# Query casts moved from GpSimd to VectorE, and a last tile's stores over two queues in place of three

## The chip, the core and the metric

The kernel runs on one core of a Trainium2 chip. A core has engines that run side by side, each through its own list of instructions in program order: TensorE (PE in the profile; it multiplies matrices, and PEld is its loading of weights), VectorE (DVE) and GpSimd (POOL) for elementwise work, ScalarE (ACT) for functions such as exp and GELU, and SyncE (SP), which here only issues transfers. Transfers (DMA) run beside the engines. The metric is the time of one execution on the device in microseconds, as the median of several runs.

## The reference

Two stages, in float32. Attention in a window of 32 positions to either side, for 8 batches of 8 heads, 576 positions and 64 features a head; then a feed-forward layer over all 4608 tokens.

```python
# q, k, v: (8, 8, 576, 64)
scores = np.matmul(q, k.transpose(0, 1, 3, 2)) / np.sqrt(64)
scores = np.where(np.abs(pos[:, None] - pos[None, :]) <= 32, scores, -1e9)
attn = softmax(scores)                                # written out in the original
x = np.matmul(attn, v).transpose(0, 2, 1, 3).reshape(4608, 512)
h = x @ w_in                                          # w_in:  (512, 2048)
g = 0.5 * h * (1 + np.tanh(c * (h + 0.044715 * h * h * h)))   # c = sqrt(2 / pi)
out = g @ w_out                                       # w_out: (2048, 512)
```

## The kernel before

The tokens are taken in 9 tiles of 512 (t = 0 to 8). In each tile a first product, `ffn_in`, makes h from the attention's output xT and puts it through GELU; a second product, `ffn_out`, multiplies by w_out. From tile 1 on the second product is done as seven half-size products in place of eight (Winograd's form), for which VectorE makes sums of quarters of g (S1 to S4) and combines the results into the output quarters C11, C12, C21 and C22. The attention of batch t + 1 is woven into the second product of tile t, by a plan of steps: s is a group of scores and its exp, m the mask, v the product with V and the reciprocal of the sums, x the scaled write into xT.

Queries and keys arrive in float32. They must be cast to float16 and turned, so that features lie on partitions. From batch 2 on the turning is done by DMA transposes, which SyncE issues:

```python
    def cast_and_turn(b):
        cast_open(b)
        q16, k16 = halfs[b]
        qr, kr, qt, kt = raws[b]
        # ...
        def queries(src, dst, p0, p1):
            for pr in range(NPAIR):                     # 4 pairs of heads
                nc.gpsimd.tensor_copy(
                    dst[:, pr, :, :, :].rearrange("p j h d -> p h j d"),
                    src[:, 2 * pr:2 * pr + 2, :].rearrange("p h (j d) -> p h j d", j=4))
            nc.sync.dma_start_transpose(QTs[b].rearrange("d r j p -> d (r j) p")[:, :, p0:p1],
                                        dst.rearrange("p r j h d -> p (r j h d)"))

        queries(qr, q16, 0, 128)
        for pr in range(NPAIR):
            nc.vector.tensor_copy(k16[:, pr, :, :, :], kr[:, :, 2 * pr:2 * pr + 2, :])
            nc.sync.dma_start_transpose(
                KTs[b % 2][:, pr, 0:512].rearrange("d (c p) -> d c p", c=4),
                k16[:, pr, :, :, :].rearrange("p c h d -> p (c h d)"))
        queries(qt, qt16, 128, 144)                     # the last 64 positions
        nc.vector.tensor_copy(kt16.rearrange("p r h d -> p (r h d)"), kt.rearrange("p h d -> p (h d)"))
        nc.sync.dma_start_transpose(
            KTs[b % 2][:, :, 512:576], kt16.rearrange("p r h d -> p (r h d)"))
```

Queries come as 128 partitions x 512 elements a pair of heads (qr) and 16 x 512 for the tail (qt). The order of the program in one tile decides what stands behind what on each engine:

```python
    for t in range(NT):
        b = t + 1
        att = b < B
        if t:
            for fc in range(begun):
                ffn_in(t, fc, 3, 4)
            if att and b > 1:
                cast_and_turn(b)
            for fc in range(begun, NF):
                ffn_in(t, fc)                           # GELU, and the sums after every fourth
        # ...
        if t and b + 1 < B:
            load_qk(b + 1)                              # SyncE: qr, four parts of kr, qt, kt
        for i in range(113 if t else 65):
            for act in plan.get(i, "").split():
                # s, m, v, x of the plan; with the first v:
                #   if t and g < 0 and b + 1 < B: load_v(b + 1)   # GpSimd: five casting loads
                ...
            # one matmul of the second product
        # ffn_last(t): the last quarter's additions and its stores
```

The scores of a pair need its part of QT and KT (line 354 of the kernel); the sums are line 490:

```python
    def gelu(t, n):
        fc = column(t, n)
        nc.scalar.activation(gTs[t][:, fc, :], phs[fc], AF.Gelu_apprx_tanh)
        if t and n % 4 == 3:
            sums(t, n // 4)

    def sums(t, i):
        # ...
        for dst, x, y, op in ((S1, A21, A22, ALU.add), (S2, S1, A11, ALU.subtract),
                              (S3, A11, A21, ALU.subtract), (S4, A12, S2, ALU.subtract)):
            nc.vector.tensor_tensor(dst, x, y, op=op)
```

Results go out from GpSimd's queue, in the last tile over several queues. `three` is used for the quarter C22 of the last tile alone; there `store` makes two transfers for the first block of 128 tokens and five for the second:

```python
    turn_about, three = [nc.sync, nc.scalar], [nc.sync, nc.gpsimd, nc.scalar]

    def store(t, t4, yo, cols=slice(0, 512), eng=None):
        # for each stretch of rows that is contiguous in the output:
            if t == NT - 1 and eng is None:
                turn_about.append(turn_about.pop(0))
            if eng is three:
                three.append(three.pop(0))
            q_ = three[0] if eng is three else eng or (turn_about[0] if t == NT - 1 else nc.gpsimd)
            q_.dma_start(out_v[b, j, q0 + p:q0 + p + e, cols], yo[m:m + e, cols])
    # ...
        elif n == 4:                                    # in ffn_out
            if not end:
                nc.vector.tensor_tensor(C22, py, U3, op=ALU.add)
            else:
                for x, part in enumerate((py[:, 0, :], pys["apart"][:, 0:256])):
                    nc.vector.tensor_tensor(C22[:, x, :], part, U3[:, x, :], op=ALU.add)
                    store(t, 2 + x, yo[:, 2 + x, :], right, three)
```

Of the kernel before, what the change touches and what calls it, by code (L numbers as in the profile page):

```python
# [29 lines left out]
def cut(b):  # L30
    return 120 if b else 128
# [30 lines left out]
def kernel(  # L62
# [9 lines left out]
    nc = tc.nc  # L72
# [5 lines left out]
    NT = NTOK // 512  # L78
# [149 lines left out]
    for i in (0, 3, 4, 1, 2):  # L228
        m, off = masks[i], 0
# [16 lines left out]
    def cast_open(b):  # L246
        halfs[b] = [hp.tile([128, NPAIR, 4, 2, 64], FP16, name="q16"),
                    hp.tile([128, NPAIR, 4, 2, 64], FP16, name="k16")]
        QTs[b] = ap_.tile([128, NPAIR, 4, 144], FP16, name="QT")
# [44 lines left out]
    def bank(i):  # L294

        return psM.tile([128, 512], FP32, name="mm", tag=f"x{i}")
# [5 lines left out]
# [4 lines that stand above are left out]
        qt16 = hp.tile([16, NPAIR, 4, 2, 64], FP16, name="qt16")  # L306
        kt16 = hp.tile([64, NPAIR, 2, 64], FP16, name="kt16")
        def queries(src, dst, p0, p1):
            for pr in range(NPAIR):
                nc.gpsimd.tensor_copy(  # L310
                    dst[:, pr, :, :, :].rearrange("p j h d -> p h j d"),
                    src[:, 2 * pr:2 * pr + 2, :].rearrange("p h (j d) -> p h j d", j=4))
            nc.sync.dma_start_transpose(QTs[b].rearrange("d r j p -> d (r j) p")[:, :, p0:p1],
# [8 lines that stand above are left out]
        queries(qt, qt16, 128, 144)  # L322
# [3 lines that stand above are left out]
# [132 lines left out]
    def first(t):  # L458

        return (t + 1) % 2  # L460
# [17 lines left out]
    def combine(i):  # L478
        dst, x, y = wino["todo"][i]
        nc.vector.tensor_tensor(dst, x, y, op=ALU.subtract)  # L480
# [11 lines left out]
    out_v = out.rearrange("(b p j) f -> b j p f", b=B, j=4)  # L492
    pys = {}

    turn_about, three = [nc.sync, nc.scalar], [nc.sync, nc.gpsimd, nc.scalar]

    def store(t, t4, yo, cols=slice(0, 512), eng=None):
        m = 0
        while m < 128:
            b, c = divmod(t * 512 + t4 * 128 + m, S)  # L500
            q0, n = (0, cut(b)) if c < 4 * cut(b) else (cut(b), 144 - cut(b))
            j, p = divmod(c - 4 * q0, n)
            e = min(n - p, 128 - m)
            if t == NT - 1 and eng is None:
                turn_about.append(turn_about.pop(0))
            if eng is three:
                three.append(three.pop(0))
            q_ = three[0] if eng is three else eng or (turn_about[0] if t == NT - 1 else nc.gpsimd)
            q_.dma_start(out_v[b, j, q0 + p:q0 + p + e, cols], yo[m:m + e, cols])  # L509
            m += e  # L510

    later = []
# [1 line left out]
    def ffn_out_0(t4, fc):  # L514
        if fc == 0:
            pys[t4] = bank(t4 % 2)
        nc.tensor.matmul(pys[t4], gTs[0][:, fc, t4 * 128:t4 * 128 + 128], w_out16[:, fc, :],
                         start=(fc == 0), stop=(fc == NF - 1))
        if fc == NF - 1:
            yo = yp.tile([128, 512], FP32, name="yo", tag="yo")  # L520
            nc.vector.tensor_copy(yo, pys[t4])
            if t4 == 3:
                store(0, t4, yo)
            else:
                later.append((t4, yo))

    def ffn_out(t, i):

        n, blk, f = i // 16, i // 8 % 2, i % 8
        if t == 1 and i > 2 and i in wino["todo"]:  # L530
            combine(i)
        a, w, new = WINO[n]
        end = t == NT - 1
        if i % 16 == 0 and new:
            pys[n % 2] = bank((first(t) + n) % 2)
            if end and n == 4:
                pys["apart"] = psO.tile([128, 512], FP32, name="py2", tag="O")
        py = pys[n % 2].rearrange("p (b c) -> p b c", b=2)
        apart = end and blk and n in (4, 6)
        if a[0] == "A":  # L540
            r0, c0 = 8 * (int(a[2]) - 1) + f, 256 * (int(a[1]) - 1) + 128 * blk
            lhsT = gTs[t][:, r0, c0:c0 + 128]
        else:
            lhsT = wino[a][:, f, 128 * blk:128 * blk + 128]
        one = end and n in (4, 6)
        nc.tensor.matmul(pys["apart"][:, 0:256] if apart else py[:, blk, :], lhsT,  # L546
                         wino[w][:, f, :], start=(new and i % (8 if one else 16) == 0),
                         stop=(i % (8 if one else 16) == (7 if one else 15)),
                         skip_group_check=True)
        if i % 16 < 15:  # L550
            return
        yo, left, right = wino["yo"], slice(0, 256), slice(256, 512)
        C11, C12, C21, C22 = (yo[:, r:r + 2, c] for r in (0, 2) for c in (left, right))

        M1, U2, U3 = C21, C12, C22
        if n == 0:
            nc.vector.tensor_copy(M1, py)
        elif n == 1:
            nc.vector.tensor_tensor(U2, py, M1, op=ALU.add)
        elif n == 2:  # L560
            nc.vector.tensor_copy(C11, py)
            if end:
                for x in range(2):
                    store(t, x, yo[:, x, :], left, nc.sync)
        elif n == 3:
            nc.vector.tensor_tensor(U3, py, M1, op=ALU.add)
        elif n == 4:
            if not end:
                nc.vector.tensor_tensor(C22, py, U3, op=ALU.add)
            else:  # L570
                for x, part in enumerate((py[:, 0, :], pys["apart"][:, 0:256])):
                    nc.vector.tensor_tensor(C22[:, x, :], part, U3[:, x, :], op=ALU.add)
                    store(t, 2 + x, yo[:, 2 + x, :], right, three)
        elif n == 5:
            nc.vector.tensor_tensor(C21, py, M1, op=ALU.add)  # L575
            for x in range(2):
                store(t, 2 + x, yo[:, 2 + x, :], left if end else slice(0, 512))
# [121 lines left out]
    for t in range(NT):  # L699
        b = t + 1  # L700
# [18 lines left out]
        for i in range(113 if t else 65):  # L719
# [33 lines left out]
            if t == 0 and i in (38, 40, 55):  # L753
                t4, yo = later.pop(0)
                store(0, t4, yo, eng=nc.scalar)
            if t == 0 and i < 64:
                ffn_out_0(*ORDER_0[i])
            elif t and i < 112:
                ffn_out(t, i)
# [36 lines left out]
```

## Time and profile before

| what | value |
|---|---|
| time, median of 3 runs | 315.29 us (314.19 to 315.38) |
| span of the profiled execution | 313.6 us |
| TensorE busy | 298.4 us, 95% |
| VectorE busy | 204.2 us, 65% |
| ScalarE busy | 200.3 us, 64% |
| GpSimd busy | 133.8 us, 43% |
| granted TensorE clock | 0.998 of full |
| end of VectorE's last addition | 308.83 us |

The profile is of one execution. Its times start at the first instruction and run to 313.6; a row of a time line gives start, duration, engine, line of the kernel, operation and what is written and read, and in brackets the idle time of the engine before it with what ended it. "xN" joins N instructions of a kind that follow each other; two that overlap in the pipeline start closer together than one lasts. "SPq" is SyncE issuing transfers. Groups give total busy time and then the mean in nanoseconds of one. An engine that isn't the bound may idle for nothing; what counts is idle time of the one that sets the end.

### The profile page before, as it was taken

What the parts mean: (1) busy time and instruction counts of PE and PEld (TensorE: products, weight loads), DVE (VectorE), ACT (ScalarE), POOL (GpSimd) and SP (SyncE); (2) the same over time, 40 slices, a digit from 0 to 9 for tenths busy, and PEclk for the clock granted to TensorE, in tenths of its full rate; (3) what the DMA queues carried; (4) which work ended last, traced back from release to release, by engine and by line L of the source; (5) the groups of instructions that cost most, each with busy time, mean ns of one, the idle gap of its engine ahead of it and who ended that gap; (6) DMA issues with size and microseconds to landing.
All of it is one profiled execution on the core that took longest, in us unless ns stands there. A gap on an engine that the chain in (4) does not pass through costs nothing.

```text
span 313.6 us, 6733 instructions
## 1 busy us (share of the span) xinstructions
PE 298.4 (95%) x2643; PEld 187.4 (60%) x2643; DVE 204.2 (65%) x405; ACT 200.3 (64%) x315; POOL 133.8 (43%) x209
## 2 busy tenths in 40 slices
PE   7789989998899999999999999999999999999993
PEld 2453535444685478547864786477646864784582
DVE  5664587749776866696669666966686653633551
ACT  1677467567667677767776867686768676706600
POOL 3557255099108910892079306930680051006001
PEclk9999999999999999999999999999999999999999
DMA  7999998999996899769975999599653022004013
GB/s 207 238 332 372 374 333 194 281 176 139 123 268 142 121 116 253 171 120 138 246 178 111 134 238 193 107 125 260 145 135 78 2 64 73 2 0 134 2 43 92
DMA packets 120035, 50.64 MB, mean 161 GB/s; under 512 B 101351, under 2 KB 113296, under 8 KB 120004
## 3 DMA queue, kind: packets, MB, share of 16 engines
q1 hardware_dynamic: 84243, 37.43, 53.4%
q0 software_dynamic: 34864, 11.63, 38.2%
q10 hardware_dynamic: 897, 1.16, 1.1%
q8 instruction: 20, 0.33, 0.5%
q14 instruction: 11, 0.09, 0.1%
HBM read 37.62 MB, written 9.44 MB: 150 GB/s over the span
## 4 chain that ended last, share of the span: by engine, by line
PE 71%; SPq 12%; DMA 12%; DVE 2%; issue 1%; ACT 1%; POOL 0%; DVEq 0%
PE mm L546 31%; PE mm L446 19%; PE ph L446 11%; SPq L139 5%; PE ps_o L387 4%; PE ps_s L354 4%; DMA KT<-k 3%; DMA wst<-in_moe_w_in_dram 3%; DMA qr<-in_q_dram 3%; PE ps_d L387 3%; SPq L162 2%; DMA kr<-in_k_dram 2%; SPq L130 1%; SPq L181 1%; DVE k L318 1%; SPq L185 1%
## 5 line engine op out<-in xcount | busy, mean ns | idle before, releaser
L509 POOL DMA_DIRECT2D out_dram<-y x80 | 43.7, 554 | 129.3 <-DVE y L575 110.9
L446 PEld LDWEIGHTS <-w_in 128*128 128x128 f16 x576 | 56.1, 98 | 66.6 <-POOL w_in L190 1.8
L446 PE MATMUL mm<-xT,w_in 128*128 128x512 f16 x352 | 86.4, 379 | 0.2 <-POOL w_in L190 0.2
L454 ACT ACTIVATE gT<-mm 128x512 f16<-128x512 f32 x88 | 52.4, 599 | 36.7 <-PE mm L446 36.7
L446 PE MATMUL ph<-xT,w_in 128*128 128x512 f16 x224 | 58.8, 379 | 0.3 <-POOL w_in L190 0.3
L490 DVE TENSOR_TENSOR s<-gT 128x512 f16<-128x512 f16 x64 | 34.6, 541 | 35.3 <-ACT gT L454 35.1
L546 PEld LDWEIGHTS <-s 128*128 128x128 f16 x512 | 48.6, 98 | 7.5
L360 ACT ACTIVATE pe<-ps_s 128x704 f16<-128x704 f32 x64 | 43.4, 729 | 9.8 <-PE ps_s L354 9.0
L546 PE MATMUL mm<-t,s 128*128 128x256 f16 x376 | 45.7, 273 | 0.0
L401 ACT ACTIVATE lt<-ps_d 128x480 f32<-128x480 f32 (+3 forms) x40 | 22.3, 556 | 32.1 <-PE ps_d L387 32.0
L454 ACT ACTIVATE gT<-ph 128x512 f16<-128x512 f32 x56 | 33.0, 599 | 13.0 <-PE ph L446 12.9
L546 PEld LDWEIGHTS <-gT 128*128 128x128 f16 x384 | 36.0, 98 | 7.3
L546 PE MATMUL mm<-w_out,gT 128*128 128x256 f16 x256 | 32.8, 273 | 0.0
L369 DVE TENSOR_TENSOR pe<-pe,mask 128x704 f16<-128x704 f16 x64 | 31.3, 526 | 1.0 <-ACT pe L360 1.0
L411 DVE TENSOR_TENSOR xT<-ps_o,lt 128x480 f16<-128x480 f32 (+5 forms) x38 | 20.2, 549 | 13.5 <-ACT lt L402 13.5
L387 PEld LDWEIGHTS <-V 128*64 128x64 f16 x336 | 18.0, 109 | 11.6 <-issue 4.4
L402 ACT ACTIVATE lt<-lt 128x480 f32<-128x480 f32 (+3 forms) x40 | 23.5, 587 | 1.3
L490 DVE TENSOR_TENSOR s<-s,gT 128x512 f16<-128x512 f16 x32 | 23.2, 726 | 1.1
L387 PE MATMUL ps_o<-pe,V 128*64 128x160 f16 (+2 forms) x244 | 21.7, 241 | 1.2 <-POOL V L263 1.2
L87 ACT ACT_TABLE_LOAD x17 | 21.8, 1283 | 1.1 <-PEq L780 0.8
L387 PE MATMUL ps_d<-pe,ones 128*64 128x192 f16 (+2 forms) x264 | 22.4, 235 | 0.0
L170 POOL DMA_DIRECT2D V<-in_v_dram x24 | 21.5, 916 | 0.0
(77 smaller groups left out, 322.0 us busy)
## 6 DMA issues: line engine op xcount, KB each, us to landing
kr<-in_k_dram SPq DMA_DIRECT2D x32, 256.0 KB, 7.7
qr<-in_q_dram SPq DMA_DIRECT2D x6, 1024.0 KB, 8.4
V<-in_v_dram POOLq DMA_DIRECT2D x30, 128.0 KB, 6.2
wst<-in_moe_w_in_dram SPq DMA_DIRECT2D x3, 1024.0 KB
wst<-in_moe_w_out_dram SPq DMA_DIRECT2D x3, 1024.0 KB, 11.2
qr<-in_q_dram SPq DMA_DIRECT2D x8, 256.0 KB
vr<-in_v_dram SPq DMA_DIRECT2D x16, 128.0 KB, 5.2
out_dram<-y POOLq DMA_DIRECT2D x24, 48.0 KB, 2.0
```

The costliest lines, as they stand in the source:

```text
L87: nc.scalar.add_instruction(mybir.InstLoadActFuncSet(name=nc.get_next_instruction_name(), act_func_set_id=which, ins=[], outs=[]))
L170: nc.gpsimd.dma_start(V[:, c, :, :], v[b, :, 128 * c:128 * c + 128, :].rearrange("h p d -> p h d"))
L360: nc.scalar.activation(pe, ps[:, :, 0:w], AF.Exp, scale=SCALE)
L369: nc.vector.tensor_tensor(pe, pe, m.rearrange("p (o w) -> p o w", o=1).broadcast_to(list(pe.shape)), op=ALU.mult)
L387: nc.tensor.matmul(bk[r0:r0 + 64, at:at + 4 * n].rearrange("d (j p) -> d j p", j=4)[:, :, p0 - q0:p1 - q0], V[:, c, 2 * pr + h, :] if w == ...
L401: nc.scalar.activation(lt[:, 0:n], d[:, 0:n], AF.Ln)
L402: nc.scalar.activation(lt[:, 0:n], lt[:, 0:n], AF.Exp, scale=-1.0)
L446: nc.tensor.matmul(ph, w_in16[:, dc, fc * 128:fc * 128 + 128], xT[:, dc, t * 512 % RING:t * 512 % RING + 512], start=(dc == 0), stop=(dc = ...
L454: nc.scalar.activation(gTs[t][:, fc, :], phs[fc], AF.Gelu_apprx_tanh)
L490: nc.vector.tensor_tensor(dst, x, y, op=op)
L509: q_.dma_start(out_v[b, j, q0 + p:q0 + p + e, cols], yo[m:m + e, cols])
L546: nc.tensor.matmul(pys["apart"][:, 0:256] if apart else py[:, blk, :], lhsT, wino[w][:, f, :], start=(new and i % (8 if one else 16) == 0) ...
```

## The change

Two things are changed. The casts of queries (qr and its tail qt) of batches 2 to 7 go from GpSimd to VectorE, at the same place in the program: four ahead of the four key casts, four between these and the cast of the keys' tail. This takes elementwise work off GpSimd, which also prepares the loads of V and the stores, and brings all casts of a batch onto one engine. And in the last tile the seven stores of C22 no longer take turns over SyncE, GpSimd and ScalarE; they take turns with the later stores over SyncE and ScalarE. The steps of the plan are the same in both kernels, and so are the products.

```diff
         def queries(src, dst, p0, p1):
             for pr in range(NPAIR):
-                nc.gpsimd.tensor_copy(
+                nc.vector.tensor_copy(
                     dst[:, pr, :, :, :].rearrange("p j h d -> p h j d"),
                     src[:, 2 * pr:2 * pr + 2, :].rearrange("p h (j d) -> p h j d", j=4))
# ...
-    turn_about, three = [nc.sync, nc.scalar], [nc.sync, nc.gpsimd, nc.scalar]
+    turn_about = [nc.sync, nc.scalar]
# ...
             if t == NT - 1 and eng is None:
-                turn_about.append(turn_about.pop(0))
-            if eng is three:
-                three.append(three.pop(0))
-            q_ = three[0] if eng is three else eng or (turn_about[0] if t == NT - 1 else nc.gpsimd)
-            q_.dma_start(out_v[b, j, q0 + p:q0 + p + e, cols], yo[m:m + e, cols])
+                turn_about.reverse()
+            (eng or turn_about[0] if t == NT - 1 else eng or nc.gpsimd).dma_start(
+                out_v[b, j, q0 + p:q0 + p + e, cols], yo[m:m + e, cols])
# ...
-                    store(t, 2 + x, yo[:, 2 + x, :], right, three)
+                    store(t, 2 + x, yo[:, 2 + x, :], right)
```

## The prediction

> **What bounds the kernel now.** I read the page's chain of work first, to learn which engine ends last; then a table of busy time by stretch of the run, cut where the tiles begin; then, only for the stretches in which TensorE isn't full, the time lines of the engines it waits for. The chain, from section 4 of the page:
>
> ```profile
> PE 71%; SPq 12%; DMA 12%; DVE 2%; issue 1%; ACT 1%; POOL 0%; DVEq 0%
> ```
>
> TensorE (PE) is most of the chain. Almost all SyncE (SPq) and DMA pieces of it lie ahead of 78 us: the loading of weights and of the first batches. The table by stretch says where TensorE is idle (tile 1 is 64.00 to 96.30, tile 2 to 128.40, tile 3 to 160.20; the columns are busy us and instruction counts of PE, weight loads, VectorE, ScalarE, GpSimd, then clock, DMA share, GB/s):
>
> ```profile
> 64.00:96.30 32.30, 29.95 (x288) 19.90 (x287) 24.55 (x46) 22.25 (x37) 16.07 (x21) 1.00 1.60 171
> 96.30:128.40 32.10, 31.89 (x298) 20.83 (x296) 23.13 (x45) 23.43 (x38) 16.02 (x25) 1.00 1.39 163
> 128.40:160.20 31.80, 31.80 (x297) 20.81 (x296) 23.06 (x44) 23.38 (x38) 16.07 (x25) 1.00 1.17 169
> ```
>
> From tile 3 on TensorE has no idle time at all (the same holds to 282 us), so nothing done for VectorE or GpSimd can shorten those tiles. Tile 1 has 32.30 - 29.95 = 2.35 us of idle time, tile 2 has 0.21 us. Ahead of 64 us the change touches nothing, because the changed function is called for batches 2 to 7 alone and first runs in tile 1. So 2.56 us is all that a better order of casts can win. TensorE's time line in tile 1 shows the idle time as two waits, both at the start of a group of score products (the brackets give the idle time before a row and what ended it):
>
> ```profile
> 77.50 0.46 PE L354 MATMUL ps_s<-QT,KT 64*128 64x160 f16 x8 [1.11 <-DMA KT<-k]
> 84.94 0.46 PE L354 MATMUL ps_s<-QT,KT 64*128 64x160 f16 x8 [1.24 <-ACT lt L402]
> ```
>
> 1.11 + 1.24 = 2.35, the whole of it. The first waits for the DMA transpose of the keys. The second is put down to ScalarE's reciprocal, which scores do not read; the score's own inputs are QT and KT of the third pair, so I take it for a transpose too (in tile 2 the same product follows the one before it without a wait). Why the transposes are late is on GpSimd's and SyncE's time lines of tile 1:
>
> ```profile
> 68.19 3.03 POOL L310 CAST q<-qr 128x512 f16<-128x512 f32 x4
> 71.17 3.04 POOL L310 CAST qt<-qt 16x512 f16<-16x512 f32 x4
> ```
>
> ```profile
> 71.25 1.83 SPq L313 DMA_TRANSPOSE QT<-q  x1
> 73.17 5.79 SPq L319 DMA_TRANSPOSE KT<-k  x4
> ```
>
> SyncE issues in program order: the query transpose stands ahead of the four key transposes, and it starts when the fourth query cast ends (71.22). GpSimd starts those casts only at 68.19, after five V loads. The waits of SyncE confirm it for all six batches:
>
> ```profile
> SPq L313 <- POOL q L310: 57.9, 6, 10.6
> ```
>
> **What the Trainium skill says.** "SBUF — State Buffer", section "Who interferes with whom": a VectorE instruction with two SBUF inputs contends with a GpSimd instruction that reads SBUF, and a cast in a two-port mode contends with GpSimd too, each blocking wholly. The trace agrees. In tile 3, with the casts on GpSimd from 133.15 to 138.57, VectorE shows
>
> ```profile
> 133.19 1.97 DVE L490 TENSOR_TENSOR s<-s,gT 128x512 f16<-128x512 f16 x1
> 135.09 0.82 DVE L490 TENSOR_TENSOR s<-gT 128x512 f16<-128x512 f16 x1
> 143.67 0.42 DVE L490 TENSOR_TENSOR s<-gT 128x512 f16<-128x512 f16 x1
> ```
>
> that is 0.42 us alone, and 0.82 to 1.97 us beside them. "VectorE: DVE Perf Modes", section "Side-by-side: where the cycles go for N=2048 bf16", gives about 150 cycles of start, 8 of fill and one cycle per two elements for a doubled mode at 0.96 GHz; for 512 elements an estimate of (256 + 8 + 150) / 0.96 = 431 ns. The key casts, of the same size and types, have a median of 420 ns, and the one early query cast on VectorE took 427. I use 0.42, and 0.36 us from start to start (1.43 us for four in tile 3).
>
> **The change, part by part.**
>
> *Removed from GpSimd:* 24 casts q and 24 casts qt, these rows of the groups kept apart by shape:
>
> ```profile
> L310 POOL CAST qt<-qt 16x512 f16<-16x512 f32 x24 | 18.2, 794 | 0.0
> L310 POOL CAST q<-qr 128x512 f16<-128x512 f32 x24 | 15.6, 695 | 0.0
> ```
>
> 18.2 + 15.6 = 33.8 us, so its busy time goes from 133.8 to about 100 us. None is on the path from tile 3 on.
>
> *Added to VectorE:* 48 casts of about 0.42, or 20.2 us. *Taken off VectorE:* the collisions. Against 0.42, the 64 sums of mean 541 lose 7.7 us, the 32 of 726 lose 9.8, the 32 of 506 lose 2.8, the 24 key casts of 491 lose 1.7: together 22 us. VectorE's 204.2 us should thus stay within 198 to 208, though it has 48 instructions more.
>
> *Moved, tile 1:* VectorE is idle from 62.76 to 66.88, waiting for the keys' load (4.12 us). The query load landed at 59.66. Four query casts, 1.4 us, fit into that gap for nothing. SyncE is free from 63.2, so the query transpose can go at about 64.3 in place of 71.25. The first key cast ends near 67.3 and the first key transpose is issued just after, in place of 73.17. Each of the four comes 5.7 us or more earlier, against waits of 1.11 and 1.24. If it lands as long after its issue as before, both waits go: -2.35 us. The qt and kt casts follow to about 70, where the sums start today (70.68).
>
> *Moved, tile 2:* the query transpose goes from 103.62 to about 98.7 (VectorE's additions end at 97.24, plus four casts); the remaining 0.21 us goes.
>
> *Tiles 3 to 6:* in tile 3 the additions end at 129.24. Thirteen casts of 0.36 take 4.7 us, to 133.9; before, the five key casts ended at 131.52. The first group of sums starts at 133.9 in place of 132.51, but runs at 0.36 each: to 135.4, where before its fourth sum ended at 136.65. The fourth group waits for the last GELU as now, at 142.87. What TensorE takes from VectorE comes no later: 0.
>
> *The end:* the seven stores of the quarter C22 of the last tile go alternately over ScalarE and SyncE; before, over GpSimd, ScalarE and SyncE in turn.
>
> ```profile
> 302.14 7.65 SPq L509 DMA_DIRECT2D out_dram<-y  x11
> 304.50 5.70 ACTq L509 DMA_DIRECT2D out_dram<-y  x8
> ```
>
> GpSimd had three of 22; now SyncE has 13 and ScalarE 9. The three lie between 304.75 and 306.64, and both other queues are idle from 306.12 to 307.38, waiting for the next quarter. Three issues of about 0.36 us fit there. The last issue (309.87, ScalarE) waits for the last additions, which end at 308.83, and for the stores shortly ahead: 0, give or take 0.3.
>
> **Sum:** -2.35 - 0.21 = -2.56. The second wait's cause is inferred; at 85% it costs 0.19 of expectation. 315.29 - 2.56 + 0.19 = 312.9 us.
>
> **The rivals.**
>
> *The keys are bound by their load and by traffic.* The last key chunk lands at 66.8 whatever the casts do. The V loads also move some 6 us earlier, with the removed casts ahead of them gone, so they still lie beside the transposes. "DMA: Bandwidth & Descriptors", section "Issuing engines are not separate DMA queues", says that transfers of all issuers share 16 DMA engines and interleave. In agreement, V loads issued in tile 1 at 74.16 and later land up to 8.3 us after their issue, and those at 63.80, without transposes beside them, 4.7 us. If the transposes take 4 us longer, they still arrive before 76.4; against this rival, then, stands 5.7 us of lead. It would leave the time near 314.5.
>
> *VectorE becomes the bound.* Its 13 casts ahead of the sums stand in program order; a query tail that lands late would stop the sums behind it. For it: VectorE already waits for keys in tile 3 (0.52 us). Against it: GpSimd never waits for these inputs now, the key tail issued after the query tail is always in time, and SyncE starts the next batch's loads some 5 us earlier. If I am wrong by 0.5 us in each of six tiles, the time is 316.
>
> *GpSimd is blocked from writing its descriptors by VectorE's casts.* In tile 3 its stores run to 133.15, beside casts. Late stores would hold the output tile, first rewritten at 144.95: 11 us of room. I give it no cost.
>
> *The end gets longer* by a queue fewer: at worst three issues in one queue, +1.1 us, or 314.0.
>
> **Range and chances.** The runs of before spread by 1.2 us, 314.19 to 315.38. All gone and a quick run is 311.6; half gone with a longer end is 314.6. A gain over 2% would need 6.3 us, more than twice the idle time there is to win: 2%. A loss over 2% needs about 1 us more in each of six full tiles: 2%. Within 2%: 96%.
>
> **What would show it.** Right: no score wait in tile 1, tile 1 near 30.0 us long with TensorE busy throughout; query transpose in tile 1 near 64 to 65; sums uniformly 0.42; GpSimd near 100 us; tiles 3 to 6 still 31.8. Wrong: a wait for KT or QT that stays; a wait of VectorE for qr or qt with sums ending after 144; tiles from 3 on longer than 31.9; the stretch from the last addition to the end over 5.0 us (now 313.6 - 308.83 = 4.8).

## The result, and the profile after

| | before | after |
|---|---|---|
| time, median | 315.19 us (314.19 to 315.38) | 311.51 us (310.69 to 312.75) |
| ratio, 95% interval | | 0.9893 (0.9853 to 0.9933) |
| span of the profiled execution | 313.56 us | 309.96 us |
| VectorE busy | 204.2 us | 198.4 us |
| GpSimd busy | 133.8 us | 104.1 us |

The change is faster by 1.1%. The forecast was 312.9 us, with a range of 311.6 to 314.6; the median lies just below the lower edge, and the ratio taken on the 315.29 of the forecast gives 311.9. The direction and most of the mechanism held; the gain was larger than the 2.4 us stated.

The chain of work of the changed kernel:

```profile
PE 78%; SPq 10%; DMA 7%; DVE 2%; issue 1%; POOL 0%; POOLq 0%
```

TensorE has gained 7 points of the chain, about what DMA (12 to 7) and SyncE (12 to 10) have lost: fewer pieces of loading and turning stand between matmuls. The busy time by stretch, tiles 1 to 3, cut up to 1 us behind the places where these tiles now begin (columns as before):

```profile
64.00:94.00 30.00, 29.64 (x287) 19.82 (x286) 23.99 (x53) 21.85 (x35) 10.70 (x13) 1.00 1.42 183
94.00:126.00 32.00, 32.00 (x298) 20.94 (x297) 22.23 (x53) 23.53 (x38) 11.28 (x17) 1.00 1.24 167
126.00:157.80 31.80, 31.80 (x298) 20.80 (x296) 21.98 (x53) 23.38 (x37) 11.14 (x17) 1.00 1.16 166
```

Idle time of TensorE in tile 1 has gone from 2.35 to 0.36 us, in tile 2 from 0.21 to nothing; tile 3 takes 31.80 as before. TensorE's time line shows the two score products that waited, now without a bracket, and what took the second wait's place:

```profile
75.47 0.47 PE L354 MATMUL ps_s<-QT,KT 64*128 64x160 f16 x8
81.61 0.46 PE L354 MATMUL ps_s<-QT,KT 64*128 64x160 f16 x8
84.61 0.26 PE L387 MATMUL ps_o<-pe,V 128*64 128x160 f16 x2 [0.36 <-DVE xT L411]
```

SyncE's time line of tile 1 has the transposes earlier, the queries' by 7.7 us and the first of the keys' by 5.2:

```profile
63.53 4.31 SPq L313 DMA_TRANSPOSE QT<-q  x1
67.93 5.69 SPq L319 DMA_TRANSPOSE KT<-k  x4
```

And VectorE's: the first four casts lie in what was its wait for keys, as forecast. The next rows are slower than forecast; tile 2 has the forecast pace again.

```profile
61.83 1.43 DVE L310 CAST q<-qr 128x512 f16<-128x512 f32 x4
65.73 2.18 DVE L318 CAST k<-kr 128x512 f16<-128x512 f32 x4 [2.46 <-DMA kr<-in_k_dram]
67.83 2.14 DVE L310 CAST qt<-qt 16x512 f16<-16x512 f32 x4
94.18 1.45 DVE L310 CAST q<-qr 128x512 f16<-128x512 f32 x4
```

Between 63.0 and 71.7 GpSimd prepares nine V loads, and four casts beside them take 2.1 to 2.2 us in place of 1.4. In the Trainium skill, the page "SBUF — State Buffer", section "Who interferes with whom", says that whichever of the two engines issues first holds the ports that they share for its whole instruction. That fits: the V loads would now do a little of what the GpSimd casts did. No run tests it apart. In the groups the sums are all at their lone speed (before: means of 541, 726 and 506 ns):

```profile
L490 DVE TENSOR_TENSOR s<-gT 128x512 f16<-128x512 f16 x64 | 26.9, 420 | 42.1 <-ACT gT L454 42.1
L490 DVE TENSOR_TENSOR s<-s,gT 128x512 f16<-128x512 f16 x32 | 13.6, 425 | 1.1
L490 DVE TENSOR_TENSOR s<-gT,s 128x512 f16<-128x512 f16 x32 | 13.4, 418 | 0.0
```

To see where time comes from, each profile is cut into five stretches: up to the start of tile 1's second product (P1), from there to that of tile 2 (W1), to that of tile 3 (W2), to the end of VectorE's last addition (rest), and from there to the end of the program (closing). All in us:

| profile | P1 | W1 | W2 | rest | closing | span |
|---|---|---|---|---|---|---|
| before | 75.57 | 34.39 | 32.08 | 166.79 | 4.73 | 313.56 |
| before again (e3) | 75.23 | 34.28 | 32.69 | 166.79 | 4.71 | 313.72 |
| stores only (e2) | 76.29 | 33.82 | 31.80 | 166.79 | 4.28 | 312.99 |
| casts only (e1) | 74.26 | 32.27 | 31.80 | 166.79 | 4.72 | 309.85 |
| casts only again (e12) | 74.07 | 32.27 | 31.80 | 166.79 | 4.80 | 309.74 |
| after | 74.72 | 32.27 | 31.80 | 166.79 | 4.37 | 309.96 |
| after again (e4) | 73.78 | 32.30 | 31.80 | 166.79 | 4.28 | 308.95 |
| GpSimd casts early (e5) | 74.61 | 32.27 | 32.76 | 166.91 | 4.75 | 311.30 |
| casts twice (e6) | 73.72 | 35.75 | 32.99 | 168.33 | 4.30 | 315.09 |
| T4 later (e7) | 75.31 | 31.90 | 31.80 | 166.79 | 4.30 | 310.10 |
| C11 from GpSimd (e8) | 74.20 | 32.32 | 31.80 | 166.79 | 4.20 | 309.31 |
| casts added behind (e9) | 74.20 | 34.85 | 31.80 | 166.79 | 4.27 | 311.92 |
| last stores from GpSimd (e10) | 74.33 | 32.31 | 31.80 | 166.79 | 6.14 | 311.38 |
| one GpSimd store (e11) | 74.25 | 32.42 | 31.80 | 166.79 | 4.49 | 309.76 |

Between the two first profiles the 3.60 us of gain are 0.85 in P1, 2.12 in W1, 0.28 in W2, 0 in the rest and 0.36 in the closing.

### The profile page after: what moved, and what is told of

Same layout as the page of the kernel before. It is cut to its first block, busy times and chain, and to the rows that moved or that the text cites. A ratio compares the mean times of both kernels' runs of the same rounds, so it can differ in the third digit from the quotient of the medians.

```text
span 310.0 us, 6731 instructions
## 1 busy us (share of the span) xinstructions
PE 298.4 (96%) x2643; PEld 187.5 (61%) x2643; DVE 198.4 (64%) x453; ACT 200.1 (65%) x315; POOL 104.1 (34%) x158
## 4 chain that ended last, share of the span: by engine, by line
PE 78%; SPq 10%; DMA 7%; DVE 2%; issue 1%; POOL 0%; POOLq 0%
PE mm L544 31%; PE mm L446 22%; PE ph L446 13%; SPq L139 5%; PE ps_o L387 4%; PE ps_s L354 3%; DMA wst<-in_moe_w_in_dram 3%; PE ps_d L387 3%; DMA qr<-in_q_dram 3%; SPq L130 2%; DMA tr<-in_k_dram 1%; PE mm L515 1%; SPq L181 1%; SPq L143 1%; SPq L185 1%
## 5 line engine op out<-in xcount | busy, mean ns | idle before, releaser
L506 POOL DMA_DIRECT2D out_dram<-y x77 | 45.2, 595 | 115.4 <-DVE y L573 114.7
L490 DVE TENSOR_TENSOR s<-gT 128x512 f16<-128x512 f16 x64 | 26.9, 420 | 42.1 <-ACT gT L454 42.1
L387 PEld LDWEIGHTS <-ones 128*64 128x64 f16 x336 | 18.6, 110 | 0.1
```

The costliest lines, as they stand in the source:

```text
L387: nc.tensor.matmul(bk[r0:r0 + 64, at:at + 4 * n].rearrange("d (j p) -> d j p", j=4)[:, :, p0 - q0:p1 - q0], V[:, c, 2 * pr + h, :] if w == ...
L506: (eng or turn_about[0] if t == NT - 1 else eng or nc.gpsimd).dma_start(out_v[b, j, q0 + p:q0 + p + e, cols], yo[m:m + e, cols])
```

## The experiments

My theory: the gain is the waits of tile 1 and 2, won by issuing transposes earlier. The rivals: the end of collisions between GpSimd and VectorE; the stores; spread of the loading at the start. Each ratio is to the kernel before, measured beside the run. "By the clock" means by these medians of many executions; a profile shows one execution only.

**e1, casts alone.** The kernel before with the query casts on VectorE; its stores keep three queues.

```diff
-                nc.gpsimd.tensor_copy(
+                nc.vector.tensor_copy(
```

> Only the query casts of batches 2 to 7 go to VectorE; the last tile's stores keep their three queues. Theory (earlier transposes take the waits of tile 1 away): no score wait in tile 1, from the start of tile 1's second product to that of tile 2's about 32.3 us in place of 34.39, ratio to before 0.991 to 0.993, that is within 0.2% of the whole change. Rival (the stores bring part of it): 0.5 us or more slower than the whole change. If the 0.85 us by which the changed kernel's profile was already ahead when tile 1's second product began comes from the change, it is there again: that product begins near 74.7; if it is only the spread of the loading, it begins anywhere from 74.5 to 76.

Measured 0.9929 (0.9907 to 0.995). W1 is 32.27 and no score waits, as the theory said. TensorE's only wait from 62 us on:

```profile
PE ps_o L387 <- DVE xT L411: 0.4, 1, 0.4
```

P1 is 74.26. The median, 312.71 us, is 1.3 us above that of the whole change measured beside it (e4, 311.45), where the rival asked for 0.5; the two intervals overlap, so this doesn't decide how much the stores bring.

**e2, stores alone.** The changed kernel with the casts on GpSimd.

```diff
-                nc.vector.tensor_copy(
+                nc.gpsimd.tensor_copy(
```

> Only the stores of the quarter C22 in the last tile go over two queues; the query casts stay on GpSimd. Theory: waits of 1.1 and 1.2 us in tile 1 stay, ratio 0.998 to 1.002; from the last addition to the end 4.4 to 4.8 us. Rival (a queue fewer shortens the end): ratio near 0.998 and an end of 4.4 us. Rival (a queue fewer lengthens it): ratio near 1.002 and an end over 5.0 us.

Measured 0.9961 (0.9943 to 0.9979), so by the clock the stores bring something here, against my forecast of nothing. TensorE's waits from 62 us on stay:

```profile
PE ps_s L354 <- DMA KT<-k: 1.1, 1, 1.1
PE ps_s L354 <- ACT lt L401: 0.6, 1, 0.6
```

The closing is 4.28, shorter by 0.43 to 0.45. The clock says 1.2 us (0.7 to 1.8); the profile shows 0.4 of it in the closing. Its W1 and W2 are shorter too, and its P1 is longer, where the stores have nothing to do.

**e3 and e4, both kernels once more**, without an edit.

> The kernel before, unchanged. Ratio 1.000 within 0.002; its profile tells how far the start of tile 1's second product (75.57 in the first profile of before, 74.72 in that of after) moves from one execution to another with no change at all: if by 0.5 us or more, the 0.85 us is spread.

> The changed kernel, unchanged. Ratio near 0.989. If the head start of 0.85 us is the change's own, tile 1's second product begins at 74.7 again and ahead of the unchanged kernel's by 0.7 to 1.0 us; if it is spread, the two profiles differ by less than 0.5 us or the other way round, and the ratio comes nearer to 0.992.

Measured 1.0007 (0.9981 to 1.0033) and 0.990 (0.9868 to 0.9931). The kernel before moves by 0.34 us in P1 between profiles and by 0.61 in W2 (its transposes of tile 2 make TensorE wait 0.20 in one and 0.82 in the other); the changed one moves by 0.94 in P1. P1 of the changed kernel was again ahead, by 1.45. That fits neither reading cleanly: 0.34 is under the 0.5 that was to mean spread, and 1.45 is over the 0.7 to 1.0 that was to mean a head start.

**e5, GpSimd casts, but early.** The kernel before, with the V loads of batch 2 behind the casts of batch 2:

```diff
                 cast_and_turn(b)
+                if b == 2:
+                    load_v(2)
 # ... at the end of tile 0
-            load_v(2)
```

> The kernel before with one change: in tile 1 GpSimd does the query casts ahead of the five V loads of batch 2, not behind them. VectorE does no query cast and the stores keep three queues. Theory (what counts is when the transposes are issued, not which engine casts): the query transpose of tile 1 is issued near 66 in place of 71, the score waits of tile 1 (2.35 us) fall to under 0.5, ratio to before 0.991 to 0.995, though VectorE's sums still collide. Rival (the collisions of GpSimd with VectorE are what costs): ratio 0.998 or more. Rival (the loading of the keys and the traffic bind the transposes): the waits stay over 1.5 us.

Measured 0.9955 (0.9936 to 0.9973), just above the 0.991 to 0.995 of the theory. GpSimd's and SyncE's time lines:

```profile
62.85 2.28 POOL L310 CAST q<-qr 128x512 f16<-128x512 f32 x4
```

```profile
65.16 1.83 SPq L313 DMA_TRANSPOSE QT<-q  x1
67.09 5.89 SPq L319 DMA_TRANSPOSE KT<-k  x4
```

With the casts still on GpSimd W1 is 32.27, the same as with VectorE's. So in tile 1 it is the time of the transposes that counts, and not the engine or the collisions. In tile 2, where nothing was reordered, a wait of 0.89 us stays. TensorE's waits from 62 us on:

```profile
PE ps_s L354 <- DMA KT<-k: 0.9, 1, 0.9
PE ps_o L387 <- DVE xT L411: 0.4, 1, 0.4
```

Tile 2 (W2) makes up 0.96 of the 1.45 us by which this profile's span exceeds e1's.

**e6, every query cast done twice on VectorE.**

```diff
-                nc.vector.tensor_copy(
+                for _ in range(2):
+                  nc.vector.tensor_copy(
# ... its two operands, indented
```

> The changed kernel with every query cast done twice on VectorE, 48 more instructions, about 17 to 20 us of its time. Theory (VectorE has slack in the first products): tiles 2 to 6 stay at 31.8 us, time within 0.2% of the changed kernel's, ratio to before 0.988 to 0.992. Rival (VectorE is close to being the bound): tiles of 32.1 us or more, 2 us or more slower than the changed kernel.

My expectation fell. Measured 1.0105 (1.0079 to 1.0132), 6.1 us more than the changed kernel's 311.45. TensorE's only waits from 62 us on:

```profile
PE ps_s L355 <- DMA KT<-k: 4.5, 4, 2.2
```

The doubled casts stand ahead of the transposes. The second profile of the changed kernel (e4) starts its second product of tile 1 at nearly the same time (P1 of 73.78, here 73.72), so the two can be laid side by side. Here the queries' transpose is issued 2.3 us later (64.64, not 62.38) and the first keys' 2.8 later (69.24, not 66.48). The first keys' transpose lands 2.2 us later, by the last of its completion marks in the trace (76.69, not 74.51), and the first score waits 2.2 us. So the delay reaches TensorE whole; the lead of 5.7 us that the forecast set against the rival of traffic was not there. About 0.7 us behind the wait the granted clock of TensorE fell as well, to 0.50 for 3.4 us:

```profile
73.70:80.00 6.30, 4.10 (x42) 2.87 (x41) 3.95 (x11) 4.14 (x6) 0.87 (x1) 0.79 1.80 152
77.40:80.80 3.40, 3.40 (x29) 2.41 (x23) 1.04 (x3) 1.97 (x4) 0.87 (x1) 0.50 1.62 180
```

**e7, T4 later.** The new wait of 0.36 us in tile 1 is put down to VectorE's write into xT. Two combinations of output weights, 1.2 us each, are in VectorE's way there:

```diff
-                           33: (T4, B21, T2)})
+                           60: (T4, B21, T2)})
```

> The changed kernel with one VectorE instruction of 1.2 us, the last combination of output weights (T4), moved in tile 1 from step 33 of the second product to step 60; it is needed at step 80. Theory (the new wait of 0.36 us in tile 1, put down to VectorE's write into xT, is VectorE being late by this instruction): that wait goes, tile 1's second product to tile 2's takes 31.9 in place of 32.28 us, ratio to before 0.988 to 0.990. Rival (the wait comes from ScalarE's reciprocal ahead of it): the wait stays at 0.3 us or more.

Measured 0.9901 (0.9878 to 0.9925). TensorE is busy without a pause in W1 now:

```profile
75.31:107.21 31.90, 31.90 (x297) 20.86 (x296) 24.23 (x57) 23.37 (x37) 11.18 (x16) 1.00 1.33 183
```

The wait was VectorE's. From P1 to the last addition no wait of TensorE over 0.15 us is left. By the profile this is the best version; its median of 311.12 us, against 311.45 of the changed kernel measured at another time, is within what the intervals leave open.

**e8, the quarter C11 from GpSimd.**

```diff
-                    store(t, x, yo[:, x, :], left, nc.sync)
+                    store(t, x, yo[:, x, :], left, nc.gpsimd)
```

> The changed kernel, but in the last tile the four stores of the quarter C11, the first to be stored, go from GpSimd in place of SyncE. GpSimd then has its last store some 2.3 us earlier than in the kernel before, and SyncE four transfers fewer. Theory (a transfer of GpSimd in the last microseconds lengthens the closing of the program, whatever it carries): from the last addition to the end 4.7 us again, as in the kernels with three queues. Rival (only the number and time of the last stores on SyncE and ScalarE counts): 4.3 us or less.

Measured 0.9908 (0.9884 to 0.9932) and a closing of 4.20 us: the theory fell. A store of GpSimd 4.9 us ahead of the last addition's end costs nothing.

**e9, eight more casts a batch, behind the transposes.** Written to a tile that is free by then (t16 of batch 1):

```diff
             KTs[b % 2][:, :, 512:576], kt16.rearrange("p r h d -> p (r h d)"))
+        for pr in 2 * list(range(NPAIR)):
+            nc.vector.tensor_copy(halfs[1][2].rearrange("p (j h) d -> p h j d", h=2),
+                                  qr[:, 2 * pr:2 * pr + 2, :].rearrange("p h (j d) -> p h j d", j=4))
```

> The changed kernel with eight more casts of queries a batch on VectorE, as many instructions as in the run that cast twice, but placed behind the last transpose of the batch and written to a tile that nobody reads. Theory (casting twice cost 2% because the transposes were issued later, not because VectorE ran out of time): no score waits for a transpose, tiles 2 to 6 stay at 31.8 us, time within 0.3% of the changed kernel's, ratio to before 0.988 to 0.993; at most 0.5 us of waiting for sums in tile 1. Rival (VectorE has no room for 48 more casts): ratio 1.005 or more, as with casting twice.

Measured 0.9999 (0.9976 to 1.0022), where the theory said 0.988 to 0.993. W1 is 34.85, 2.6 us longer than in the changed kernel. TensorE's waits from 62 us on, all in tile 1:

```profile
PE mm L547 <- DVE s L493: 1.1, 1, 1.1
PE ps_o L390 <- DVE xT L420: 0.9, 1, 0.9
PE ps_o L390 <- DVE xT L414: 0.4, 1, 0.4
```

No score is listed as waiting, and tiles 2 to 6 are as in the changed kernel (31.80 to 31.87) with eight casts more in each. So VectorE has room for eight more casts in every tile but the first, where it must wait for keys until 64.56 and the added eight take 4.73 us beside the V loads. Casting twice, by contrast, lengthened W2 and the rest as well, by late transposes. The theory and the rival of e6 were each half right: in tile 1 VectorE has no slack of this size, elsewhere the place ahead of the transposes is what is dear.

**e10, the last quarter's first stores from GpSimd.**

```diff
-                store(t, x, yo[:, x, :], right, nc.scalar if x else nc.sync)
+                store(t, x, yo[:, x, :], right, nc.scalar if x else nc.gpsimd)
```

> The changed kernel, but the last quarter's two stores of the first block go from GpSimd in place of SyncE. Theory (the closing of the program waits for GpSimd's drain, which ends about 5.0 us after GpSimd's last store is issued, and SyncE's drain follows that by 1.0 us): GpSimd's last store is issued near 0.2 us after VectorE's last addition, its drain ends near 5.2, and the program 7.1 us after the addition in place of 4.3, so 2.8 us slower than the changed kernel, ratio to before 0.998 to 1.001. Rival (GpSimd's stores cost no more than others): 4.3 to 4.9 us and a ratio of 0.989 to 0.991.

Measured 0.9975 (0.9955 to 0.9994), and a closing of 6.14 us, 1.8 longer than after; the theory's 7.1 was too much. A drain is an instruction at the end of the program, here on GpSimd's queue (POOLq). The groups of the closing (durations in ns, smallest, median and largest; then first and last start) show it:

```profile
L789 POOLq DRAIN  x3: 46/102/5509, 305.1 to 311.1; - x3
```

It lasts 5.5 us, ends 5.36 after the last addition, and the program ends 0.78 after that. In the kernel before it is as long and began at 306.0:

```profile
L791 POOLq DRAIN  x3: 46/102/5567, 306.0 to 313.3; - x3
```

There it ends 2.78 after the last addition, ahead of SyncE's last wait for a store. So the drain can set the end, as in e10, but in the kernel before it ended ahead of the last landing of a store (2.94) and didn't. What is longer with three queues is the stretch from that landing to the end of SyncE's own drain: 0.95 us in place of 0.66 after. In the trace, SyncE goes through six more checks of semaphores behind that landing, where the changed kernel has three, some 0.06 us each, and its drain takes 0.12 us in place of 0.01; a pause of 0.39 us is in both. Why its drain is longer is open.

**e11 and e12, one GpSimd store, and the casts alone once more.** In e11, with the casts on VectorE, GpSimd leaves the turn after its first store of C22:

```diff
             q_.dma_start(out_v[b, j, q0 + p:q0 + p + e, cols], yo[m:m + e, cols])
+            if eng is three and q_ is nc.gpsimd:
+                three.remove(nc.gpsimd)
```

> The run with only the casts moved, but GpSimd takes just the first of the seven stores of C22; the other six alternate over SyncE and ScalarE. GpSimd's last store is then issued about 4.1 us ahead of the end of VectorE's last addition in place of 2.7. Theory (GpSimd's drain, some 5.6 us long in the profile and perhaps longer without it, is what three queues cost): from the last addition to the end 4.3 us, ratio to before 0.989 to 0.991, as the whole change. Rival (the 1.2 us by which the clock favours two queues is the spread of executions and not the stores): the ratio equals that of the casts alone in this same job, within 0.001.

> The run with only the casts moved, unchanged, beside the run with one store on GpSimd. Theory: 0.9925 to 0.9935 again and 4.7 us from the last addition to the end, some 1 us slower than with one store on GpSimd. Rival: the same as that run within 0.001, anywhere from 0.989 to 0.994.

Measured 0.9923 (0.99 to 0.9945) and 0.9918 (0.9889 to 0.9948): the same, as the rival said, though the closings are 4.49 and 4.80. The 1.2 us that the clock gave the stores in e2, and the 1.3 between e1 and e4, did not come back here, though e11 still has one of GpSimd's three stores. How much the stores bring by the clock stays open; what the profiles show each time is a closing 0.3 to 0.5 us shorter.

## Why the prediction was right, and where a size was off

*What bounds the kernel, and the path.* Right. TensorE sets the end; the rest, tiles 3 to 8, is 166.79 us in all profiles but e5 and e6.

*Tile 1, -2.35.* The mechanism is shown by e1 and e5; measured -2.12. Both waits are gone, the second too, so it was indeed a transpose that it waited for: with transposes issued 5 us earlier, by either engine, it vanishes. In the kernel before, the third key transpose lands at 84.90 and the product starts at 84.94. The second profile of that kernel (e3) puts all its waits, two in tile 1 and one in tile 2, down to key transposes:

```profile
PE ps_s L354 <- DMA KT<-k: 3.1, 3, 1.1
```

The missing 0.23 us is the new wait of 0.36 behind VectorE's weight combinations (shown by e7), less 0.13 of matmuls that run closer together. The forecast hadn't named it. It doesn't come from the query casts: e5, which has none of them on VectorE, shows the same wait.

*Tile 2, -0.21.* -0.28 between the first two profiles, -0.89 against the second profile of before. The term was sized from one execution, and this wait varies with the traffic; it is zero in every profile with casts on VectorE ahead of the transposes, save the doubled ones.

*VectorE's cost and the collisions.* Inside the range, at its lower edge: forecast 198 to 208, measured 198.4, with the sums at 0.42 again. Their end brings no time in tile 1 (e5 keeps the collisions and gains as much there). The pace of 0.36 us a cast was wrong for the key and tail casts of tile 1, where V loads lie beside: 0.55. On the other side GpSimd's busy time fell by 29.7 us where 33.8 were forecast: its V loads took 942 ns each (before, 916) and its stores 595 (554). No wait of TensorE comes from that.

*The lead.* Wrong in size; that it was enough is luck. Transposes were issued 7.7 and 5.2 us earlier, but SyncE took 4.31 us to issue the first where it had taken 1.83, and 1.83 again in e5, where GpSimd prepared no V load beside it. The first key transpose then took longer to land as well: 7.1 us from its issue, where it had taken 4.3, and 3.1 in e5. It landed at 75.02 for a product that starts at 75.47. In the nine profiles with each query cast made once on VectorE ahead of the transposes, that product starts 0.05 to 0.77 us behind this landing, in six of them by 0.06 or less. The kernel before, which waits, has the same 0.05 (77.45 and 77.50). In e5, with the V loads behind the casts, it is 5.2 us. So the rival of traffic took nearly the whole lead for the first pair of heads, and e6 shows what a later landing costs. The third pair's transpose, landing at 77.99 for a product at 81.61, had 3.6 us to spare. Casts on VectorE together with later V loads were not run.

*The end, 0 give or take 0.3.* Mis-sized: -0.36 and -0.43 in the profiles of the changed kernel. The last store is issued as long after the last addition as forecast (0.97 us, was 1.04); the saving is behind it.

*P1, not forecast.* 0.85 us between the first profiles. Up to the first query cast, near 62 us, the two programs are the same on every engine. (That cast starts at 61.83, so the forecast's "ahead of 64 us the change touches nothing" was 2 us off; the 0.85 us were there by then.) The loss in the kernel before lies between 41 and 45 us, in VectorE's wait for output weights. VectorE in the kernel before, then in the changed one:

```profile
42.10 1.18 DVE L190 CAST w_out<-wst 128x512 f16<-128x512 f32 x2 [1.05 <-DMA wst<-in_moe_w_out_dram]
```

```profile
40.83 1.18 DVE L190 CAST w_out<-wst 128x512 f16<-128x512 f32 x2 [0.20 <-DMA wst<-in_moe_w_out_dram]
```

P1 is 74.6 to 76.3 in the four profiles with casts on GpSimd and 73.7 to 75.3 in the ten with casts on VectorE. They overlap, but the difference of the means is 1.1 us, and the wait for output weights shown above doesn't overlap at all: 0.78 to 1.05 us in the four, 0.20 to 0.69 in the ten. Whether it is chance or something in the changed programs that the profile doesn't show stays open; no run tests it. By the clock the casts alone bring 2.2 and 2.6 us (0.9929 and 0.9918 of 315.1 and 314.5), which W1 and W2 can account for without P1.

Of the sum, then: -2.56 stood for -2.40 (W1 and W2 of the first two profiles), 0 for -0.36 (closing), and nothing for -0.85 (P1).

## What to carry to other kernels

Where an in-order queue of transfers feeds the bound engine, ask when its first entry can be issued, and move the work ahead of it to an engine that is idle just then, or to an earlier place on its own engine; which engine is faster matters less. Count a lead at its end, where the data land and not where the transfer is issued, and with the traffic that the same change sets free: here an issue 5.2 us earlier left 0.05 to 0.77 us to spare at the product. Test it by delaying the step: a landing 2.2 us later brought a wait of 2.2 us. Slack isn't one number for an engine: the same eight casts were free in tiles 2 to 6, cost 2.6 us in tile 1, and cost more in several tiles when put ahead of the transposes.

## What the runs showed of the hardware

GpSimd's drain after its last store took 5.35 to 5.96 us in these kernels, and held the end of the program when that store was issued 0.06 us ahead of the end of the last addition (e10). And TensorE's granted clock, 1.00 throughout tile 1 in the kernel before with two waits of 1.1 and 1.2 us, fell to 0.50 for 3.4 us behind a single wait of 2.2 us (e6). TensorE's busy time in W1 was then 33.55 us in place of 31.92, so 1.6 us were lost beyond the wait itself. This is one execution. Behind TensorE's other waits of 0.9 us or more once it had started, of which the longest was 1.24, the clock stayed at 1.00.
